# adaLN block (attention, then a gated spatial MLP): where the second half of the modulation vector is computed

## The chip, the cores and the metric

The kernel runs on one core of a Trainium2 chip. The metric is the time of one execution on the device in microseconds. All data are float32; TensorE is fed with float32 and with a rounded float32 form (F32R) of the same size.

## The reference, cut to what matters

Six modulation vectors of 448 numbers come from one vector `c` and one matrix; they scale and shift the two layer norms and gate the two branches:

```python
mod = (_silu(c) @ w_mod).reshape(c.shape[0], 6, 1, -1)        # c: 1x448, w_mod: 448x2688
sa, ca, ga, sb, cb, gb = (mod[:, i] for i in range(6))
h = _layernorm(x) * (1 + ca) + sa                             # x: 1x2048x448
x = x + ga * attention(h, A_wqkv, A_wo)                       # 16 heads of 28, 2048 keys
h = _layernorm(x) * (1 + cb) + sb
x = x + gb * gmlp(h, B_w_in, B_w_sp, B_b_sp, B_w_out)         # w_sp: 2048x2048
```

`sa` and `ca` are needed before anything else can be computed. `ga` is multiplied into the rows of `A_wo`, `gb` into those of `B_w_out`, and `sb`, `cb` are needed by the second norm, behind the attention.

## The kernel before

The order of the work is written out by hand: each engine runs its instructions in the order in which the program issues them, and semaphores join the engines. SP (SyncE) issues nearly all loads and stores, in one queue. The stages, by the time of the profile, are these.

**QKV, 0 to about 150 us.** The first norm's columns `sa`, `ca` (tiles `cols`, one column for each 128 channels, channel on the partition) are made from the first third of `w_mod` (`load_mod_chunk`, `mod_sum`, `mod_mul`, `mod_add`, `mod_prod`). Then, for four groups of 512 tokens, `ln_next` transposes the normed tokens, `v_tile` makes the values of 128 tokens, and `qk_unit` makes 128 rows of q and k for a group and sends them to memory (`qk_store` on SP). The other two thirds of `w_mod` are loaded by `load_mod` (pairs 1 and 2; four tiles of 112x896 each, SP). `mod_acc` on VectorE multiplies each of the four tiles with its column of `silu` and adds them up in `acc`, 112 channels on the partitions. What is left is a sum over 112 partitions, made on TensorE with a matrix of ones: `mod_bc` (L261) gives a gate as a row on all 128 partitions, which VectorE copies to `bcs`, and `mod_col` (L256) gives a column tile, five small matmuls, which VectorE copies to `cols`. Pair 1 (`ga`, `sb`) is finished in group 2, between two `v_tile`; pair 2 (`cb`, `gb`) behind the last `v_tile`. Each takes a bank of PSUM from the ring by `bank("pc")`: without a kind, a bank is of kind "s" (three banks) or "m" (four), by a counter `turn` that goes round seven places. The heads' tiles are three pairs, `kst` and `qst` (`stk`); `pads` clears their padding rows on VectorE and GpSimd (L545 to L547), then `load_head` reads a head back from memory. In the rest of the stage `qk_unit` runs with `m_first` in between, which begins the attention's maxima.

**Attention, about 150 to 870 us.** The loop over `u` has 16 heads of 16 slots; a slot is one block of 128 keys of a head. It is

```python
for u in range(NU + 1):
    for fn, a in events.pop(u, []):
        fn(*a)
    j = u + LEAD
    for qb in range(4 if u < NU else 0):
        s_mm(u, qb)
        if j < NU:
            m_mm(j, qb)
    if u % 2 == 0 and u > 0:
        pv_mm(u - 2)
        pv_mm(u - 1)
```

`s_mm` (L637) is one score tile of 128x512 on TensorE, in a bank of kind "s", and its Exp on ScalarE (L641), which reads the bank. `m_mm` (L607) is a product 20 slots ahead whose row maximum VectorE takes (L612), in a bank of kind "m". Since a kind's banks are used in turn, a score waits for the Exp of the score three before it. `pv_mm` (L652) multiplies the exponentials with the values, for two slots at once, behind each even slot. So one round is an odd slot, an even slot and then P times V.

What else happens in attention hangs on `events`: `at(slot, fn, ...)` issues `fn` ahead of the scores of that slot, in the order of the `at` calls. Before the change these are the loading of heads, the division by the softmax's sums (`n_copy` to `n_scatter`), the sums of blocks of `w_sp` (`ws_load` on SP, `ws_add` on GpSimd three slots later, L780, `ws_store`), the gated `A_wo` (`wo_load` from slot 120, `wo_prep` on GpSimd from slot 124 multiplies with `bcs["ga"]`), and the gated `B_w_out` (`wout_raw` from slot 196, `wout_prep` from slot 199 multiplies with `bcs["gb"]`). The tiles of `stage2` named "ql" have two buffers, used by `qk_unit`, then by `wo_load` and `wout_raw`. ScalarE has Exp alone in nearly all of attention; `qk_rest` at slot 3 puts one copy (L337) there.

**Behind it,** 870 to 1399 us: the output projection, the second norm (it reads `cols["sb"]`, `cols["cb"]`), the gated MLP with its large product with `w_sp`, and the output. The change doesn't touch these.

Of the kernel before, what the change touches and what calls it, by code (L numbers as in the profile page):

```python
# [30 lines left out]


@with_exitstack
def tile_adaln_mha_gmlp(ctx, tc, x, wqkv, wo, w_in, w_spT, b_sp, w_out, cT, w_mod, out):
# [129 lines left out]
    def bank(name, kind=None):  # L164

        if kind is None:
            kind = "smsmsmm"[turn[0] % 7]
            turn[0] += 1
        return ring.tile([128, 512], F32, name=name, tag=kind, bufs=3 if kind == "s" else 4)

    def load_mod(pair, eng):
        for k in range(4):
            wms[pair, k] = e1.tile([112, 2, D], F32, name="wm", tag=("wm", "wm", "raw")[pair], bufs=4)
            a = (pair * 4 + k) * 2 * D
            eng.dma_start(wms[pair, k], w_mod[:, a : a + 2 * D].rearrange("p (a b) -> p a b", b=D))

    def load_mod_chunk(c, eng):
        n = 128 if c < 3 else 64
        if c in (0, 2):
            ts = [e1.tile([112, 2 * D], F32, name="wm", tag="wm", bufs=4)[:, :512] for _ in range(2)]  # L180
        elif c == 1:
            ts = [stage.tile([128, 512], F32, name="wmc", tag="qh")[0:112] for _ in range(2)]
        else:
            ts = [stage2.tile([128, 512], F32, name="wmc", tag="ql")[0:112]]
        wms[0, c] = []
        a = c * 1024
        for t in ts:
            eng.dma_start(t, w_mod[:, a : a + 512])
            wms[0, c] += [t[:, j : j + 2 * n] for j in range(0, 512, 2 * n)]
            a += 512  # L190

    def load_x(g, eng):
        xg = e1.tile([128, 4, D], F32, name="xg")
        for t0, t1 in ((0, 1), (1, 2), (2, 4)) if g == 0 else ((0, 4),):
            eng.dma_start(xg[:, t0:t1, :], x[g, :, t0:t1])
        for t in range(4):
            xts[4 * g + t] = xg[:, t, :]
# [44 lines left out]
    accs = {}  # L242

    def mod_acc(pair, k):
        if k == 0:
            accs[pair] = e2.tile([112, 2, D], F32, name="acc")
        wm, acc = wms.pop((pair, k)), accs[pair]
        if k == 0:
            dve.tensor_scalar(out=acc, in0=wm, scalar1=silu[:, 0:1], scalar2=None, op0=ALU.mult)
        else:  # L250
            dve.scalar_tensor_tensor(out=acc, in0=wm, scalar=silu[:, k : k + 1], in1=acc, op0=ALU.mult, op1=ALU.add)

    def mod_col(nm, acc, plus1):
        pc = bank("pc")
        for c, r, e in ((0, 0, 128), (1, 0, 128), (2, 0, 128), (3, 0, 64), (3, 64, 128)):
            pe.matmul(pc[r:e, c : c + 1], acc[:, c * 128 : c * 128 + e - r], ones[:112, 0:1], start=True, stop=True)  # L256
        dve.tensor_scalar(out=cols[nm], in0=pc[:, 0:4], scalar1=plus1, scalar2=None, op0=ALU.add)

    def mod_bc(nm, acc):
        pc = bank("pc")  # L260
        pe.matmul(pc[:, :D], ones[:112, :], acc, start=True, stop=True)  # L261
        dve.tensor_copy(bcs[nm], pc[:, :D])

    mv1, xn1 = {}, {}

# [236 lines left out]
        qk_part("a", i, pool)  # L502
    for i in (0, 2, 1, 3):
        load_w("b", i, sp)
    load_mod(1, sp)
    for a in pvs:
        v_copy(*a)
    ln_stat(1, (0, 1))
# [3 lines left out]
    ln_rs(1, 2, 4)  # L512
    ln_norm(1, (2, 3))
    load_x(3, sp)
    ln_stat(2, range(4))
    turn[0] = 5
    qk_unit((0, 3), 0)
# [13 lines left out]
    qk_unit((2,), 0)  # L531
    for i in (0, 2, 1, 3):
        qk_part("b", i, dve)
    load_mod(2, sp)
    for g in range(1, NG):
        if g == 3:
            early.close()
            stk = att.enter_context(tc.tile_pool(name="stk", bufs=1))
            kq = [[stk.tile([128, S], F32R, name=f"{n}st{i}") for n in "kq"] for i in range(3)]
            kst, qst = [a[0] for a in kq], [a[1] for a in kq]  # L540
            npool = att.enter_context(tc.tile_pool(name="npool", bufs=2))

            def pads(i, eng):

                dve.memset(kst[i][64:128, :].bitcast(F32), 0.0)  # L545
                eng.memset(qst[i][64:128, :].bitcast(F32), 0.0)
                pool.memset(kst[i][64:86, :].bitcast(F32), 1.0)  # L547

            pads(0, dve)

            def load_head(h, c0=0, c1=S):
                k, q = kst[h % 3], qst[h % 3]
                if h > 2:
                    sp.dma_start(q[84:86, :].bitcast(F32), q[86:88, :].bitcast(F32))
                for r0, i in ((0, 0), (56, 1), (28, 0)):
                    sp.dma_start(k[r0 : r0 + 28, c0:c1].bitcast(F32), qk_scr[i][D + h * DH : D + (h + 1) * DH, c0:c1])
                for r0, i in ((0, 0), (28, 1), (56, 0)):
                    sp.dma_start(q[r0 : r0 + 28, c0:c1].bitcast(F32), qk_scr[i][h * DH : (h + 1) * DH, c0:c1])

            load_head(0, 0, 1536)  # L560
            for m in (0, 3):
                qk_unit((m,), g)
            load_head(0, 1536, S)
        v_tile(4 * g)
        v_tile(4 * g + 1)
        if g == 3:
            pads(1, pool)
            pads(2, pool)
        if g + 1 < NG:
            ln_next(g + 1)  # L570
        for k in range(2):
            v_tile(4 * g + 2 + k)
            if g == 2 and k == 0:
                mod_bc("ga", accs[1][:, 0, :])
                mod_col("sb", accs[1][:, 1, :], 0.0)
            if g < 3:
                mod_acc(g, k)
        if g < 3:
            for k, m in enumerate((0, 3)):
                qk_unit((m,), g)  # L580
                mod_acc(g, 2 + k)
    mod_col("cb", accs[2][:, 0, :], 1.0)
    mod_bc("gb", accs[2][:, 1, :])
    late_e.close()


# [202 lines left out]
    def at(slot, fn, *a, when=events):  # L789
        when.setdefault(slot, []).append((fn, a))  # L790
# [639 lines left out]
```

## Time and profile before

| what | us |
|---|---|
| median of 3 runs | 1400.98 (1400.81 to 1401.15) |
| the profiled execution, its own time | 1400.88 |
| span in it, first to last instruction | 1399.0 |
| TensorE busy | 1392.6 |
| VectorE busy | 1019.4 |
| ScalarE busy | 774.9 |
| GpSimd busy | 289.1 |

The profile's times are those of one execution. PE is TensorE's matmuls, PEld its weight loads, DVE VectorE, ACT ScalarE, POOL GpSimd, SPq the queue of SP. A row of a timeline is start, duration, engine, line, operation, output <- inputs, shape, count, and in brackets the idle time ahead of it with what ended it. A row of the chain is start, duration, engine, what was written, line, count.

### The profile page before, as it was taken

To read this page: it belongs to the slowest core of one execution; us is meant where nothing else is said; L and a number is where in the kernel's file an instruction comes from. 1 tells how busy PE (TensorE), PEld (TensorE's weight loads), DVE (VectorE), ACT (ScalarE), POOL (GpSimd) and SP (SyncE) were. 2 spreads that over 40 slices of the span, in tenths; PEclk is the share of its full clock that TensorE was granted. 3 is DMA by queue.
4 is the path that set the end of the run, shared out by engine and by line. 5 is a ranking of instruction groups with operands and counts; after the bars stand their busy time and mean duration, and the time that the engine had idled before them with its cause. 6 is when DMAs were issued, how large, how long until landed. Compare 5 with 4: busy or idle time off the path is not lost.

```text
span 1399.0 us, 20203 instructions
## 1 busy us (share of the span) xinstructions
PE 1392.6 (100%) x7208; PEld 992.1 (71%) x7208; DVE 1019.4 (73%) x1747; ACT 774.9 (55%) x1491; POOL 289.1 (21%) x275
## 2 busy tenths in 40 slices
PE   9999999999999999999999999999999999999998
PEld 8888655555555555555555555988998888888888
DVE  7788888888888888888888860751356655767473
ACT  5623666677777777666677779363234544434211
POOL 3043212211224143313211231000142430000000
PEclk9999999999999999999999999999999999999999
DMA  9563645555456546654434211534103333446453
GB/s 262 153 194 148 184 116 166 168 162 161 151 168 176 150 164 182 177 161 147 120 94 113 63 50 54 179 115 140 53 0 114 106 112 113 144 136 215 136 177 107
DMA packets 102669, 193.43 MB, mean 138 GB/s; under 512 B 17110, under 2 KB 32086, under 8 KB 100022
## 3 DMA queue, kind: packets, MB, share of 16 engines
q1 hardware_dynamic: 100138, 188.30, 44.4%
q10 hardware_dynamic: 2430, 3.84, 0.7%
q8 instruction: 57, 0.93, 0.3%
q14 instruction: 44, 0.36, 0.1%
HBM read 133.63 MB, written 53.67 MB: 134 GB/s over the span
## 4 chain that ended last, share of the span: by engine, by line
PE 99%; DVE 1%; ACT 0%; issue 0%; POOL 0%; POOLq 0%
PE st_ps L637 18%; PE o_ps L652 17%; PE mt L607 17%; PE acc L1204 6%; PE acc L1206 6%; PE acc L1205 6%; PE z_ps L1130 5%; PE z_ps L1016 5%; PE pq L313 5%; PE wo_ps L886 3%; PE pv L298 2%; PE y_ps L1306 2%; PE y_ps L1305 2%; PE y_ps L1307 2%; PE tp L118 1%; PE wu L240 1%
## 5 line engine op out<-in xcount | busy, mean ns | idle before, releaser
L612 DVE TENSOR_REDUCE pm<-mt 128x1 f32<-128x512 f32 x1024 | 631.0, 680 | 84.4 <-PE mt L607 83.9
L641 ACT ACTIVATE P<-st_ps 128x512 f32<-128x512 f32 x1024 | 514.4, 633 | 205.0 <-PE st_ps L637 205.0
L637 PE MATMUL st_ps<-qst,kst 128*128 128x512 f32 x1024 | 404.2, 406 | 0.2 <-DVE qf L319 0.2
L607 PE MATMUL mt<-kst,qst 128*128 128x512 f32 x1024 | 402.8, 393 | 0.1
L637 PEld LDWEIGHTS st_ps<-qst,kst 128*128 128x128 f32 x1024 | 191.3, 188 | 137.9 <-issue 93.9
L652 PE MATMUL o_ps<-P,V 128*32 128x512 f32 x2048 | 247.1, 598 | 0.0
L607 PEld LDWEIGHTS mt<-kst,qst 128*128 128x128 f32 x1024 | 192.4, 188 | 36.1 <-DVE pm L612 3.1
L780 POOL TENSOR_TENSOR ws_raw<-ws_raw 128x512 f32<-128x512 f32 x80 | 103.0, 1288 | 356.8 <-DMA ws_raw<-in_w_spT_dram 355.0
L1092 ACT ACTIVATE wsp_h<-raw_sp 128x512 fp32r<-128x512 f32 x112 | 70.2, 632 | 162.8 <-PE acc L1206 118.8
L85 DVE TENSOR_TENSOR wsp_l<-raw_sp,wsp_h 128x512 fp32r<-128x512 f32 x112 | 80.5, 729 | 90.6 <-ACT wsp_h L1092 87.8
L652 PEld LDWEIGHTS o_ps<-P,V 128*32 128x32 f32 x2048 | 54.7, 109 | 122.9 <-issue 114.6
L1204 PE MATMUL acc<-wsp_h,heapA 128*128 128x512 f32 x224 | 87.3, 390 | 0.0
L1205 PE MATMUL acc<-wsp_l,heapA 128*128 128x512 f32 x224 | 87.2, 389 | 0.0
L1206 PE MATMUL acc<-wsp_h,heapA 128*128 128x512 f32 x224 | 87.2, 389 | 0.0
L1205 PE MATMUL acc<-wsp_l,heapB 128*128 128x512 f32 x174 | 67.7, 389 | 0.0
L1206 PE MATMUL acc<-wsp_h,heapB 128*128 128x512 f32 x174 | 67.7, 389 | 0.0
L1204 PE MATMUL acc<-wsp_h,heapB 128*128 128x512 f32 x174 | 67.7, 389 | 0.0
L313 PE MATMUL pq<-heapD,heapD 128*128 128x512 f32 x196 | 62.4, 392 | 0.0
L1134 DVE BATCH_NORM_STATS2 stz<-z 128x6 f32<-128x448 f32 x32 | 19.9, 625 | 50.4 <-ACT z L1133 30.0
L1204 PEld LDWEIGHTS acc<-wsp_h,heapA 128*128 128x128 f32 x224 | 42.0, 188 | 8.9 <-DVE cD L1210 0.3
L1206 PEld LDWEIGHTS acc<-wsp_h,heapA 128*128 128x128 f32 x224 | 42.0, 188 | 8.8
L1205 PEld LDWEIGHTS acc<-wsp_l,heapA 128*128 128x128 f32 x224 | 42.0, 188 | 8.6
(219 smaller groups left out, 1595.4 us busy)
## 6 DMA issues: line engine op xcount, KB each, us to landing
ws_raw<-in_w_spT_dram SPq DMA_DIRECT2D x160, 256.0 KB
ws_scr<-ws_raw SPq DMA_DIRECT2D x80, 256.0 KB
raw_sp<-ws_scr SPq DMA_DIRECT2D x80, 256.0 KB
kst<-qk_scr SPq DMA_DIRECT2D x45, 224.0 KB
qst<-qk_scr SPq DMA_DIRECT2D x45, 224.0 KB
raw_sp<-in_w_spT_dram SPq DMA_DIRECT2D x32, 256.0 KB
qk_scr<-qh SPq DMA_DIRECT2D x28, 256.0 KB
qk_scr<-ql SPq DMA_DIRECT2D x28, 256.0 KB
```

The source lines that it names most:

```text
L85: eng.tensor_tensor(out=dst, in0=a, in1=hi.bitcast(F32), op=ALU.subtract)
L313: pe.matmul(pq, wqk[:, b, m * 128 : (m + 1) * 128], hT[g][:, a, :], start=j == 0, stop=j == NST - 1)
L607: pe.matmul(mt, qst[h % 3][:, t * 128 : (t + 1) * 128], kst[h % 3][:, kb * 512 : (kb + 1) * 512], start=True, stop=True)
L612: dve.tensor_reduce(out=pms[h][:, t, kb : kb + 1], in_=mt, axis=AX.X, op=ALU.max)
L637: pe.matmul(st, kst[h % 3][:, kt * 128 : (kt + 1) * 128], qst[h % 3][:, qb * 512 : (qb + 1) * 512], start=True, stop=True)
L641: act.activation(p, st, AF.Exp, scale=SCALE)
L652: pe.matmul(otile[h][32 * qb : 32 * qb + 32, :], V[:, kt, h, :], ptiles.pop((u, qb)), start=kt == 0, stop=kt == NT - 1)
L780: pool.tensor_tensor(out=a, in0=a, in1=b, op=SUMS[i // 16][2])
L1092: act.activation(hi, raw, AF.Copy)
L1204: pe.matmul(acc[i], zh, hi, start=st == 0, stop=False)
L1205: pe.matmul(acc[i], zh, lo, start=False, stop=False)
L1206: pe.matmul(acc[i], zl, hi, start=False, stop=st == 7)
```

## The change

`load_mod`, `mod_acc`, `mod_col` and `mod_bc` go, with all their calls; at the two places where `mod_bc` and `mod_col` took banks the counter goes on by 2. The four late vectors are made in attention instead. The host lays out their part of `w_mod` with channels on the rows: for each of `gb`, `sb`, `cb`, `ga` four tiles of 128 channels by 448 inputs (the last has its 64 channels twice). Early in QKV, SP writes `silu` to memory and reads it back as a row on all 128 partitions, into the tile of `bcs["ga"]`. In attention, for tile `i` of 16: at slot 8 + 6i SP loads it into a "ql" buffer, at slot 12 + 6i GpSimd multiplies it with the row, and at slot 16 + 6i ScalarE copies it in place and gives the sum along each row, which is one column of the vector. `sb` goes straight to `cols["sb"]`; GpSimd adds 1 to `cb`; the two gates are written to memory and read back as rows (SP; `gb` at slot 36 and `ga` at slot 108). Their column tiles are those of `sa` and `ca`.

```diff
-    def load_mod(pair, eng):
-        for k in range(4):
-            wms[pair, k] = e1.tile([112, 2, D], F32, name="wm", tag=("wm", "wm", "raw")[pair], bufs=4)
-            a = (pair * 4 + k) * 2 * D
-            eng.dma_start(wms[pair, k], w_mod[:, a : a + 2 * D].rearrange("p (a b) -> p a b", b=D))
...
+    def row(i):
+        return m_scr[0, i, 0:D].rearrange("(o n) -> o n", o=1).broadcast_to([128, D])
...
-    def mod_acc(pair, k):
...
-    def mod_col(nm, acc, plus1):
...
-    def mod_bc(nm, acc):
...
-    load_mod(1, sp)
...
     load_x(3, sp)
+    sp.dma_start(m_scr[0, 0, 0:D].rearrange("(k p) -> p k", p=112), silu)
+    sp.dma_start(bcs["ga"], row(0))
...
-    load_mod(2, sp)
...
         for k in range(2):
             v_tile(4 * g + 2 + k)
             if g == 2 and k == 0:
-                mod_bc("ga", accs[1][:, 0, :])
-                mod_col("sb", accs[1][:, 1, :], 0.0)
-            if g < 3:
-                mod_acc(g, k)
+                turn[0] += 2
         if g < 3:
-            for k, m in enumerate((0, 3)):
+            for m in (0, 3):
                 qk_unit((m,), g)
-                mod_acc(g, 2 + k)
-    mod_col("cb", accs[2][:, 0, :], 1.0)
-    mod_bc("gb", accs[2][:, 1, :])
+    turn[0] += 2
...
+    LATE = ("gb", "sb", "cb", "ga")
+    gcols = {"sb": cols["sb"], "cb": cols["cb"], "gb": cols["sa"], "ga": cols["ca"]}
+    mods = {}
+
+    def mod_load(i):
+        mods[i] = stage2.tile([128, D], F32, name="w_late", tag="ql")
+        sp.dma_start(mods[i], w_late[i])
+
+    def mod_mult(i):
+        pool.tensor_tensor(out=mods[i], in0=mods[i], in1=bcs["ga"], op=ALU.mult)
+
+    def mod_sum_row(i):
+        nm, c = LATE[i // 4], i % 4
+        m = mods.pop(i)
+        act.activation(m, m, AF.Copy, accum_out=gcols[nm][:, c : c + 1])
+
+    def mod_end(nm):
+        if nm == "cb":
+            pool.tensor_scalar(out=cols[nm], in0=cols[nm], scalar1=1.0, scalar2=None, op0=ALU.add)
+        elif nm != "sb":
+            g, r = gcols[nm], m_scr[0, 1, 0:D]
+            sp.dma_start(r[0:384].rearrange("(c p) -> p c", p=128), g[:, 0:3])
+            sp.dma_start(r[384:D].rearrange("(c p) -> p c", p=64), g[0:64, 3:4])
+            sp.dma_start(bcs[nm], row(1))
...
+    for i in range(16):
+        at(8 + 6 * i, mod_load, i)
+        at(12 + 6 * i, mod_mult, i)
+        at(16 + 6 * i, mod_sum_row, i)
+    for i, nm in enumerate(LATE):
+        at(36 + 24 * i, mod_end, nm)
```

The number of output elements, of heads and of slots stays as it was; so does every line of the stages behind attention.

More of the change, by code (lines that the diff above doesn't have):

```diff
@@ L33, in tile_adaln_mha_gmlp @@
 @with_exitstack
-def tile_adaln_mha_gmlp(ctx, tc, x, wqkv, wo, w_in, w_spT, b_sp, w_out, cT, w_mod, out):
+def tile_adaln_mha_gmlp(ctx, tc, x, wqkv, wo, w_in, w_spT, b_sp, w_out, cT, w_mod, w_late, out):
     nc = tc.nc
@@ L240, in pe_fill @@
             pe.matmul(wu[:, 0:128], with_[:, 0:128], ones, start=True, stop=True)
-    accs = {}
-    def mod_acc(pair, k):
[L245 to L251, printed above, removed]
-    def mod_col(nm, acc, plus1):
[L254 to L257, printed above, removed]
-    def mod_bc(nm, acc):
-        pc = bank("pc")
-        pe.matmul(pc[:, :D], ones[:112, :], acc, start=True, stop=True)
-        dve.tensor_copy(bcs[nm], pc[:, :D])
     mv1, xn1 = {}, {}
@@ L1401 @@
     from concourse.bass_utils import run_bass_kernel_spmd as _run
-    wm = _np.asarray(inputs["w_mod"]).reshape(4, 112, 3, 2, 448).transpose(1, 2, 0, 3, 4)
-    w_mod = _np.concatenate(
-        [wm[:, 0, :, :, c : c + 128].reshape(112, -1) for c in (0, 128, 256, 384)] + [wm[:, 1:].reshape(112, -1)], axis=1
-    )
+    wm = _np.asarray(inputs["w_mod"]).reshape(448, 6, 448)
+    first = wm[:, 0:2].reshape(4, 112, 2, 448).transpose(1, 0, 2, 3)
+    w_mod = _np.concatenate([first[..., c : c + 128].reshape(112, -1) for c in (0, 128, 256, 384)], axis=1)
+    rows = _np.concatenate([_np.arange(448), _np.arange(384, 448)])
+    w_late = wm[:, [5, 3, 4, 2]].transpose(1, 2, 0)[:, rows].reshape(16, 128, 448)
     lay = {
@@ L1416 @@
         "w_mod": w_mod,
+        "w_late": w_late,
     }
```

## The prediction

> **What bounds the kernel now.** I read the page's head and its chain of work that ended last first.
>
> ```profile
> span 1399.0 us, 20203 instructions
> PE 1392.6 (100%) x7208; PEld 992.1 (71%) x7208; DVE 1019.4 (73%) x1747; ACT 774.9 (55%) x1491; POOL 289.1 (21%) x275
> PE 99%; DVE 1%; ACT 0%; issue 0%; POOL 0%; POOLq 0%
> ```
>
> TensorE carries 99% of the chain, so the span changes by what TensorE gains or loses. The reader should distrust two things here: a TensorE busy all the time may still be waiting for very short times, because ends of matmuls are modelled, and ScalarE's 55% is a mean over stages. So the next views are the chain and the timeline at the two places that the change touches: 55 to 92 us, where the products leave TensorE, and a piece of attention, where the row sums go in. The chain, window 55 to 92 us (start, us, what):
>
> ```profile
> 59.58 2.24 PE pv L298 x11
> 61.81 0.76 PE pc L261 x2
> 62.57 0.77 PE pc L256 x10
> 63.34 2.44 PE pv L298 x11
> 65.78 10.02 PE pq L313 x44
> 75.81 8.96 PE pv L298 x44
> 84.77 0.78 PE pc L256 x10
> 85.55 0.95 PE pc L261 x2
> 86.49 0.23 PE pq L313
> ```
>
> There is no other engine in it: the products (L261, L256) stand as pieces of TensorE's own time. In attention, the chain (first two rows of its kind) and the timelines of ScalarE and VectorE show a fixed rhythm:
>
> ```profile
> 403.80 1.85 PE o_ps L652 x16
> 409.55 1.85 PE o_ps L652 x16
> ```
> ```profile
> 400.37 4.03 ACT L641 ACTIVATE P<-st_ps 128x512 f32<-128x512 f32 x8 [1.72 <-PE st_ps L637]
> 406.12 4.03 ACT L641 ACTIVATE P<-st_ps 128x512 f32<-128x512 f32 x8 [1.72 <-PE st_ps L637]
> ```
> ```profile
> 400.60 4.87 DVE L612 TENSOR_REDUCE pm<-mt 128x1 f32<-128x512 f32 x8 [0.87 <-PE mt L607]
> ```
>
> Every two slots take 409.55 - 403.80 = 5.75 us: a burst of eight scores (L637), eight products for the row maxima (L607), then P times V (L652). ScalarE makes its eight Exp in 4.03 us and rests 1.72. (Which slots these are will matter below: the burst at 158.87, quoted there, is that of slots 3 and 4, and 42 bursts of 5.75 later is 400.37, so this is the burst of slots 87 and 88.) It looks as if ScalarE had room. Whether it has room inside the burst is decided by the scores' banks: three of kind "s", so the eighth score can only be loaded when the fifth Exp has ended, the seventh after the fourth. Four close looks at one burst: weight loads on TensorE, then the fourth Exp, then the fifth.
>
> ```profile
> 402.26 0.19 PEld L607 LDWEIGHTS mt<-kst,qst 128*128 128x128 f32 x1
> 402.49 0.19 PEld L637 LDWEIGHTS st_ps<-qst,kst 128*128 128x128 f32 x1
> 402.71 0.19 PEld L607 LDWEIGHTS mt<-kst,qst 128*128 128x128 f32 x1
> 402.98 0.19 PEld L637 LDWEIGHTS st_ps<-qst,kst 128*128 128x128 f32 x1
> ```
> ```profile
> 401.82 0.62 ACT L641 ACTIVATE P<-st_ps 128x512 f32<-128x512 f32 x1
> ```
> ```profile
> 402.30 0.63 ACT L641 ACTIVATE P<-st_ps 128x512 f32<-128x512 f32 x1
> ```
>
> The fourth Exp ends at 401.82 + 0.62 = 402.44 and the seventh score's load begins 0.05 later; the fifth ends at 402.93 and the eighth load begins at 402.98, again 0.05 later. That last load comes 0.08 after the load before it ended (402.71 + 0.19), the seventh 0.04 after its own. So TensorE already waits some 0.04 us for ScalarE at the end of the burst. **ScalarE's slack in the middle of a burst is nothing**, though it is idle 30% of the time. This is the fact on which the forecast rests.
>
> **The change part by part.**
>
> *Removed from TensorE.* Without the products the two value tiles that take 2.24 us each (59.58, and 63.34 less its start-up) would follow directly: 65.78 - 59.58 - 2 x 2.24 = 1.72 us. At the second place 86.49 - 84.77 = 1.72 us. Together **-3.44 us**. Is the second 1.72 collected? The first product for the maxima (L607, 86.6 us) needs head 0 back from memory, and that load waits for pads made by VectorE:
>
> ```profile
> 72.10 1.14 DVE L251 SCALAR_TENSOR_TENSOR acc<-wm,silu,acc 112x896 f32<-112x896 f32 x1
> 73.72 1.76 DVE L545 MEMSET kst<- 64x2048 f32 x1 [0.49 <-DVE acc L251]
> ```
>
> The pad at 73.72 waited for the accumulation before it, which goes too, so it comes at least as much earlier as TensorE does. I count the full 3.44 and keep 1.72 as the other end.
>
> *Removed elsewhere.* Eight accumulations, two row copies and two column copies on VectorE, and eight loads from SP, in a stage where TensorE never waits for them: 0. Bank turns are kept by the two steps of the counter.
>
> *Added early.* SP writes silu out and reads it back as rows while the first q and k tiles are made. SP has a wait of one write in it, and behind it stand the q and k stores, which nobody needs before head 0 is loaded at 74 us: 0. If that cover were gone, one landing, about the 2.9 us that I take below for such a wait.
>
> *Added in attention, off the bound.* Per sixth slot one load on SP and one product on GpSimd. GpSimd's time by size from the row below is 1.30 x 448/512 = 1.14 us, 16 of them 18 us in 276 us where its page share is 21%. The product doesn't slow VectorE's maxima: their 4.87 us above stands beside the sum at 400.31. The question is only whether each product is ready for its sum.
>
> ```profile
> 396.05 0.81 SPq L776 DMA_DIRECT2D ws_raw<-in_w_spT_dram  x2
> ```
> ```profile
> 400.31 1.30 POOL L780 TENSOR_TENSOR ws_raw<-ws_raw 128x512 f32<-128x512 f32 x1 [3.52 <-DMA ws_raw<-in_w_spT_dram]
> ```
>
> From issue to the operation that uses a load of twice the bytes: 4.26 us. A slot is 5.75/2 = 2.87 us; SP runs up to about two slots late: this pair belongs to slot 84, two bursts before slot 88, whose first Exp begins at 402.30, so near 390.8, and it was issued 5.3 us behind that. Load to product has four slots (11.5 us) and product to sum another four: 5.7 + 4.3 + 1.1 = 11.1 of 23 us. SP's write-and-read of a finished gate, at slots 36 and 108, holds SP for a landing; its nearest row, in the view of SP's waits (in total, times, longest), is
>
> ```profile
> SPq L678 <- DMA r_scr<-rt: 7.3, 4, 2.9
> ```
>
> 2.9 us at most, behind which stand weight-sum loads, head loads (ten slots ahead of use) and the next load: still inside 23 us. GpSimd's addition of 1 to a column tile has four elements a partition. Together 0.
>
> *Added in attention, on ScalarE.* Each of the 16 sums is queued at slot 16 + 6i, always even, ahead of that slot's Exp. A burst is an odd slot and then an even one, P times V behind it, so the sum stands **between the fourth and fifth Exp**, the place without slack. Behind it queue the fifth to eighth Exp, and the eighth score waits for the fifth. Each sum therefore delays TensorE by its whole length X, and the rest of ScalarE after the burst doesn't give it back, because the next burst starts from TensorE's end. What is X? Rows of ScalarE early in the span:
>
> ```profile
> 12.23 0.56 ACT L342 ACTIVATE wv<-raw 128x448 fp32r<-128x448 f32 x1
> 12.70 0.25 ACT L413 ACTIVATE col_ca<-pc,ones 128x1 f32<-128x1 f32 x1
> 12.84 0.16 ACT L414 ACTIVATE col_sa<-pc 128x1 f32<-128x1 f32 x1
> ...
> 17.27 0.56 ACT L342 ACTIVATE wv<-raw 128x448 fp32r<-128x448 f32 x1
> 17.74 0.39 ACT L384 ACTIVATE acc<-wmc,silu 112x128 f32<-112x128 f32 x1
> ```
>
> A 128x448 copy from SBUF to SBUF lets the next instruction start 0.47 us later. The row sum has no row here: the trace holds no activation with a sum. It can't be nothing or below, since the sum has to pass 448 elements through the engine, and the fastest pace here is the Exp's own, by size 0.49 x 448/512 = 0.43 us (0.49 is (4.03 - 0.63)/7, an Exp lasting 0.63), so X is at least 0.43. Its upper end is a copy that overlaps nothing and a read-out that costs the longer 128x1 row: 0.56 + 0.25 = 0.81. I take 0.47 plus a read-out between the two 128x1 rows (0.16, 0.25), 0.21, because a sum can be written only after its last element: X = 0.68. 16 x 0.68 = **+10.9 us**.
>
> Copy between Exps: the trace has one, at slot 3, in the rest after a burst, and the page of groups has two table loads in all, neither in attention.
>
> ```profile
> 156.71 0.62 ACT L337 ACTIVATE qh<-qf 128x512 fp32r<-128x512 f32 x1
> 158.87 4.03 ACT L641 ACTIVATE P<-st_ps 128x512 f32<-128x512 f32 x8 [1.53 <-PE st_ps L637]
> ```
> ```profile
> L230 ACT ACT_TABLE_LOAD x1 | 1.3, 1283 | 0.7 <-PEq L1418 0.7
> L1020 ACT ACT_TABLE_LOAD x1 | 1.3, 1283 | 0.0
> ```
>
> That copy cost nothing (the next burst again takes 4.03), as it stood where ScalarE rests. The Trainium skill, "Perfetto Trace Analysis", section "Matmuls", says that matmul groups should go round different PSUM banks so that emptying one overlaps the next group's matmuls. By that rule the sums would be hidden under the 1.72 us of rest; the trace agrees only in so far as the banks suffice, and three do not in the burst (0.05 us behind the Exp).
>
> *Sum:* 1400.9 (the profiled execution's own time, 1399.0 of span and 1.9 around it) - 3.4 + 10.9 = 1408.4 us. The runs' median, 1400.98, is 0.1 from that execution, so the forecast stands for both.
>
> **The rivals.**
>
> *The banks leave room* (the other side). The mechanism is the ring of score banks: if the eighth score could start before the fifth Exp ends, the sum would go into ScalarE's rest and only -3.4 stays: 1397.5. It decides at a slack of X; half a slack gives a time within 0.2%. For it: 1.72 us of rest per burst, and the harmless copy at slot 3. Against it: the two distances of 0.05 us. 8% in full, 4% in part (X under 0.39, where 16 X - 3.4 is under 2.8).
>
> *The gain is not collected.* The chunk before 86 us ends on head 0's load instead: half of the gain goes, 1400.9 - 1.7 + 10.9 = 1410.1. Against it: the pad row above. 6%.
>
> *Late products.* SP's order, with its new waits on ScalarE and on a written gate, brings loads later than 23 us, and ScalarE waits inside a burst. With one slot each for the five sums nearest to SP's late slots: 5 x 2.9 = 14.5 more, 1422.9. For it: SP is two slots late already at places. Against: 12 us in hand. 5%.
>
> *Table loads.* Were Copy and Exp in two sets, each sum would cost two loads: 32 x 1.28 = 41 us, 1449. Against it: slot 3 has none. 1%.
>
> **How the numbers follow.** The forecast has 76%. Its ends: 16 x 0.43 - 3.4 = +3.5, 1404.4; and 16 x 0.81 - 1.7 = +11.3, 1412.2, which takes in the uncollected gain. That range holds 82%. A measurement of this kernel tells about 0.2%, 2.8 us, from no change. Faster 8%, within 4%, slower 88% (76 + 6 + 5 + 1).
>
> **What would show it.** Right: rows of the sum on ScalarE at even slots with nothing of L251, L256, L261 before 90 us; P times V beginning 0.7 us later in 16 bursts, the eighth score's load right behind the fifth Exp in each, and the other bursts at 5.75. The chain would name ScalarE for pieces in these bursts. The first score, whose row is here, should start 3.4 us earlier; 1.7 would mean the uncollected gain.
>
> ```profile
> L637 PE MATMUL st_ps<-qst,kst x1024: 387/393/504, 149.9 to 866.0; 128*128 128x512 f32 x171
> ```
>
> Late products would show as ScalarE idle before the sum with GpSimd as the releaser. Wrong: the 16 bursts as long as the others, or a sum shorter than 0.43 us.

## The result, and the profile after

| kernel | median us | runs |
|---|---|---|
| before | 1400.89 | 4, 1400.66 to 1401.15 |
| changed | 1423.03 | 4, 1420.17 to 1427.25 |

The changed kernel takes 1.016 times the time of before (95% interval 1.0128 to 1.0192). The sign was as forecast, the size was not: 22 us more, not 7.5. The profiled execution of the changed kernel took 1420.33 us, so its span stands 19.5 us above that of before. The page's head and its shares of the chain that ended last:

```profile
span 1418.5 us, 20212 instructions
PE 1398.0 (99%) x7184; PEld 989.5 (70%) x7184; DVE 1012.5 (71%) x1735; ACT 784.3 (55%) x1523; POOL 309.1 (22%) x292
PE 90%; DMA 4%; ACT 3%; DVE 1%; SPq 1%; issue 1%; POOL 1%; POOLq 0%; ACTq 0%
```

TensorE carried 99% of the chain before. Now 4% of it is DMA and 1% SP, and ScalarE has only 3%. So the transfers come first below, and then the sums. (In the changed kernel a score is L632, its Exp L636, a value tile L273, a q or k row L288.)

I put the start of each slot's first score side by side in the two traces and went through the differences:

| where | us | what |
|---|---|---|
| 42 to 57 us, first stage | +8.7 | one stop |
| 57 us to the first score | -3.4 | products gone from TensorE |
| slots 17, 23, ... 107 | +7.0 | 16 steps of 0.44, the sums |
| slots 45 to 48 | +3.4 | one stretch, beside a sum's step |
| slot 112 | +2.7 | one step |
| behind attention | +1.2 | small pieces, see below |

**The stop.** TensorE's timeline from 42 us, first of the kernel before, then of the changed one:

```profile
41.93 1.91 PE L118 MATMUL tp<-ident,xn 128*128 128x128 f32 x16
43.60 4.74 PE L298 MATMUL pv<-wv,heapD 128*128 128x448 f32 x22
48.17 0.86 PE L313 MATMUL pq<-heapD,heapD 128*128 128x512 f32 x3
```
```profile
42.00 1.47 PE L118 MATMUL tp<-ident,xn 128*128 128x128 f32 x12
49.14 1.11 PE L118 MATMUL tp<-ident,xn 128*128 128x128 f32 x4 [5.66 <-DVE ql L85]
50.73 6.29 PE L273 MATMUL pv<-wv,heapD 128*128 128x448 f32 x22 [0.47 <-DVE ql L85]
56.85 0.39 PE L288 MATMUL pq<-heapD,heapD 128*128 128x512 f32 x1
```

The two kernels are level at 42 us and 8.7 apart at the next q row. TensorE sits idle for 5.66 and 0.47 us, and the 22 value matmuls behind that take 6.29 us instead of 4.74. The chain of waits of the changed kernel names what stands behind VectorE's `ql`:

```profile
31.18 10.82 DMA m_scr<-silu
...
42.01 0.33 SPq L490
...
43.38 5.57 DMA qk_scr<-qh
```

Read from below: TensorE waited for VectorE's `ql`, and the chain goes from that through ScalarE's `qh` to the store of a `qh`: neither engine could go on with q and k while their buffers were still being stored. Those stores were issued late because SP stood at L490 with the read of silu; and that read waited 10.8 us for the write of silu, 1.8 KB. Not all of this is the write's own: the load of `x` (896 KB) was issued 0.4 us ahead of it in the same queue, and silu_write_16B below shows how much of the wait passes with that load.

**The removal.** The same chain of the changed kernel at the two places where the products were:

```profile
68.28 4.49 PE pv L273 x22
72.77 10.02 PE pq L288 x44
82.79 8.97 PE pv L273 x44
91.76 0.23 PE pq L288
```

The 22 value matmuls up to the 44 of q and k take 4.49 us, where from 59.58 to 65.78 us before it was 6.20: 1.71 us gone. At the end 91.76 - 82.79 = 8.97 against 86.49 - 75.81 = 10.68, again 1.71.

**A sum.** ScalarE's timeline in one burst, then the last weight loads of that burst on TensorE:

```profile
414.38 2.07 ACT L636 ACTIVATE P<-st_ps 128x512 f32<-128x512 f32 x4 [1.72 <-PE st_ps L632]
416.30 0.60 ACT L616 ACTIVATE w_late<-w_late 128x448 f32<-128x448 f32 x1
416.77 0.22 ACT L616 ACTIVATION_READ_ACCUMULATOR w_late<-w_late 128x1 f32 x1
416.86 2.08 ACT L636 ACTIVATE P<-st_ps 128x512 f32<-128x512 f32 x4
```
```profile
417.53 0.19 PEld L632 LDWEIGHTS st_ps<-qst,kst 128*128 128x128 f32 x1 [0.61 <-ACT P L636]
417.64 0.19 PEld L577 LDWEIGHTS mt<-kst,qst 128*128 128x128 f32 x1
```

The sum stands between the fourth and the fifth Exp, and the eighth score's load waits 0.61 us for the fifth Exp. The sum costs ScalarE 416.86 - 416.30 = 0.56 us: the read-out of 0.22 starts 0.47 behind it and the next Exp 0.09 behind the read-out's start, so the Exp overlaps most of the read-out. TensorE then follows with the next load 0.11 us behind instead of the usual 0.23, which gives back 0.1 of it; the step is 0.44. The view of waits over 160 to 500 us counts all of them:

```profile
PEld st_ps L632 <- ACT P L636: 9.5, 16, 0.6
```

**The gates.** SP's two longest waits on one transfer in attention (200 to 520 us; total, times, longest) and the chain behind the first of them:

```profile
SPq L625 <- DMA m_scr<-col_ca: 9.3, 1, 9.3
SPq L625 <- DMA m_scr<-col_sa: 8.3, 1, 8.3
```
```profile
265.78 8.86 DMA m_scr<-col_sa
...
275.57 8.21 DMA rb<-r_scr
...
294.89 3.05 DMA qst<-nf
...
298.08 0.47 PE st_ps L632
```

The read of the finished gate holds SP for 8.3 us, the row of softmax sums `rb` behind it lands 8.2 us after its issue, and the rest of that head's queue is late until the maxima `nf` of the next head reach their tile `qst`: TensorE waits for them at slot 48. One of the added products (1.15 us on GpSimd, L611) stands in this chain too, behind the product with `rb`.

### The profile page after: what moved, and what is told of

Read it like the earlier page. It is cut to its first block, busy times and chain, and to the rows that moved or that the text cites. A ratio compares the mean times of both kernels' runs of the same rounds, so it can differ in the third digit from the quotient of the medians.

```text
span 1418.5 us, 20212 instructions
## 1 busy us (share of the span) xinstructions
PE 1398.0 (99%) x7184; PEld 989.5 (70%) x7184; DVE 1012.5 (71%) x1735; ACT 784.3 (55%) x1523; POOL 309.1 (22%) x292
## 4 chain that ended last, share of the span: by engine, by line
PE 90%; DMA 4%; ACT 3%; DVE 1%; SPq 1%; issue 1%; POOL 1%; POOLq 0%; ACTq 0%
PE st_ps L632 16%; PE o_ps L647 16%; PE mt L577 14%; PE acc L1205 6%; PE acc L1207 6%; PE acc L1206 6%; PE z_ps L1131 5%; PE z_ps L1017 5%; PE pq L288 4%; ACT P L636 3%; PE wo_ps L887 3%; PE pv L273 2%; PE y_ps L1307 2%; PE y_ps L1308 2%; PE y_ps L1306 2%; DMA m_scr<-silu 1%
## 5 line engine op out<-in xcount | busy, mean ns | idle before, releaser
L636 ACT ACTIVATE P<-st_ps 128x512 f32<-128x512 f32 x1024 | 516.8, 629 | 208.8 <-PE st_ps L632 208.8
L632 PE MATMUL st_ps<-qst,kst 128*128 128x512 f32 x1024 | 406.1, 408 | 7.7 <-DMA qst<-nf 4.6
L632 PEld LDWEIGHTS st_ps<-qst,kst 128*128 128x128 f32 x1024 | 191.3, 188 | 150.6 <-issue 99.3
L288 PE MATMUL pq<-heapD,heapD 128*128 128x512 f32 x196 | 62.1, 390 | 0.0
```

Source lines behind the costliest of these rows:

```text
L288: pe.matmul(pq, wqk[:, b, m * 128 : (m + 1) * 128], hT[g][:, a, :], start=j == 0, stop=j == NST - 1)
L632: pe.matmul(st, kst[h % 3][:, kt * 128 : (kt + 1) * 128], qst[h % 3][:, qb * 512 : (qb + 1) * 512], start=True, stop=True)
L636: act.activation(p, st, AF.Exp, scale=SCALE)
```

## The experiments

Theory A: the detours through memory cost so much because small writes hold SP and the transfers behind them; the sums cost 0.44 us each because of their place. Each edit is against the changed kernel where nothing else is said. Where no number of runs is given there was one; the four runs of the changed kernel lie 7 us apart, so the steps in the profile say more than such a single time. The runs of before beside them had medians of 1400.7 (the first four), 1401.46 (the next four), 1401.42 (small_pieces_moved, silu_write_16B) and 1400.44 (the last two).

### silu_read_late: SP no longer waits for silu

```diff
     sp.dma_start(m_scr[0, 0, 0:D].rearrange("(k p) -> p k", p=112), silu)
-    sp.dma_start(bcs["ga"], row(0))
...
     load_head(1)
+    sp.dma_start(bcs["ga"], row(0))
```

> One move: SP reads silu's row back behind head 1's load (near 90 us) and not right behind its write at 31 us; the write stays. Theory A (SP, waiting in its queue for the landing of the small write, holds back the q and k stores, their two buffers stay full, and TensorE stops): the stop of 5.9 us ahead of the transposes near 49 us goes, the first score starts at 146.5 to 147.5 us and not at 155.2, and the whole is 8 to 9 us shorter than the changed kernel, 1411 to 1414. Rival B (the loss of that stage is the added traffic itself, or work that VectorE and GpSimd do in another order): write and read are still there, so the first score stays within 1.5 us of 155.2.

1418.46 us in one run; the first score came at 152.43, between the two theories. SP's wait is gone, but TensorE still sits idle for 3.6 us there, against 6.1. The chain:

```profile
31.38 13.96 DMA qk_scr<-qh
```

The q store issued right behind the small write, without any wait in SP, lands 14 us later (here too the load of `x` stands ahead of both). So the write delays what stands behind it in two ways: through SP when SP waits for it, and in the transfers themselves when it does not.

### sums_odd_slots: the sums moved by one slot

```diff
-        at(16 + 6 * i, mod_sum_row, i)
+        at(17 + 6 * i, mod_sum_row, i)
```

> One move: the 16 row sums on ScalarE are issued one slot later, at odd slots, so ahead of the first Exp of a burst and not between the fourth and the fifth. Theory A (a sum costs TensorE time only in the middle of a burst, where the banks of the scores leave no slack; after P times V ScalarE rests 1.72 us): the 16 steps of 0.44 us go, about 7 us, no burst of slots 17 to 107 waits for an Exp longer than before the change. Rival B (each sum's 0.56 us of ScalarE is paid wherever it stands, or the product on GpSimd is what the burst waits for): the steps stay at 0.3 to 0.6 us each, in another place of the burst.

1417.03 us. All 16 steps are gone. ScalarE around one sum:

```profile
411.60 4.03 ACT L636 ACTIVATE P<-st_ps 128x512 f32<-128x512 f32 x8 [1.72 <-PE st_ps L632]
415.43 0.65 ACT L616 ACTIVATE w_late<-w_late 128x448 f32<-128x448 f32 x1
415.90 0.27 ACT L616 ACTIVATION_READ_ACCUMULATOR w_late<-w_late 128x1 f32 x1
417.35 1.09 ACT L636 ACTIVATE P<-st_ps 128x512 f32<-128x512 f32 x2 [1.19 <-PE st_ps L632]
```

Ahead of an odd slot the sum stands where ScalarE rests: eight Exp run through in 4.03 us, and 1.19 us of idle time is left behind the read-out. In this execution the gates' stretches were dearer (5.7 us at slots 48 and 49 and 5.0 at 112 and 113, against 3.4 and 2.7), each with a stretch of half clock behind its stop: the granted clock was 0.50 from 297.5 to 300.9 us and 0.51 from 485.2 to 488.6 us, where the changed kernel had 1.00. So the span fell by 3.3 and not by 7.0.

### gate_read_late: the gates read nine slots after they are written

```diff
-            sp.dma_start(bcs[nm], row(1))
+    def mod_read(nm):
+        sp.dma_start(bcs[nm], row(1))
...
+        if nm in ("gb", "ga"):
+            at(45 + 24 * i, mod_read, nm)
```

> One move: the two finished gates are read back as rows nine slots behind their writes (slots 45 and 117) and not right behind them (36 and 108); the writes stay. Theory A (SP waits 8 to 9 us for the small writes and then reaches the store of the negated maxima late, for which the next head's scores wait): the extra steps at slots 45 to 48 (3.4 us) and 112 (2.7 us) go, about 6 us in all. Rival B (the writes' 448 elements of 4 bytes hold up the loads of heads and blocks by themselves): the steps stay.

1415.03 us. The stretch at slots 45 to 48 is gone, and the step at slot 112 is down from 2.7 to 0.6. No sum stands there (the last is at slot 106); TensorE waits 0.5 us for `nf`. So most of what the gates' detour cost here came from SP waiting in it, and a rest at slot 112 stays without that wait.

### three_moves: the three edits above together

> All three moves at once. Theory A (three separate losses, each undone by its own move, and a gain of 3.4 us from the products that left TensorE): 1397 to 1399 us, faster than the kernel before by 2 to 4 us. Rival B (a loss moves on to the next wait when one is undone, or the added loads and products cost something themselves): 1400 or more.

Four runs had a median of 1406.39 us (1405.43 to 1406.93), 1.0043 times before (1.0026 to 1.006). Attention is flat but for 0.6 us at slots 126 and 127, and the first score is still 4.0 us later than before. The view of TensorE's waits from 30 to 60 us, and behind it a stretch of the engines' busy times (PE, PEld, DVE, ACT, POOL, each with its instructions; then granted clock, DMA share, GB/s):

```profile
PE tp L118 <- DVE ql L85: 3.5, 1, 3.5
```
```profile
49.00:52.00 3.00, 3.00 (x10) 2.65 (x9) 2.93 (x8) 2.97 (x6) 0.00 (x0) 0.50 0.49 185
```

The full recovery that theory A promised failed: the small write alone, with nobody waiting for it, still stops TensorE. The next four runs ask why.

### four_moves: silu also written later

Against three_moves:

```diff
-    sp.dma_start(m_scr[0, 0, 0:D].rearrange("(k p) -> p k", p=112), silu)
...
+        if g == 1:
+            sp.dma_start(m_scr[0, 0, 0:D].rearrange("(k p) -> p k", p=112), silu)
```

> The three moves, and silu's small write itself moved from 31 us to behind the q and k stores of the second group (near 58 us), where SP has some 11 us without a store. What the earlier runs left: with only the read moved, the q store issued right behind the small write still landed 14 us later. Theory A (the small write holds up whatever lies behind it among the DMAs for about 10 us, whether or not SP waits; TensorE stops when that is a q or k store): no stop near 45 us, first score at 146.5, 1397 to 1398 us in all, faster than before by 3 to 4. Rival B (the stop near 45 us comes from the stores of the first group being late for another reason, such as the load of x ahead of them): the stop of about 4 us stays, 1403 to 1406.

1399.91 us in 11 runs (1398.79 to 1401.68), 0.9986 times before (0.9977 to 0.9995), above the range of theory A. Written behind the stores of group 1, the same pieces make no stop in the first stage, and the first score comes 2.2 us earlier than before. Of the 1.2 us that are missing from 3.4, the start-up of this execution has 0.6; the other 0.6 are lost near 115 us, as in every profile here in which silu is read back behind head 1's load. What remains are 1.3 us at slots 47 and 48, where the write of `gb` makes the next head's `nf` late, and 0.3 at slot 112.

### three_moves_16B: silu written at its old place in fewer pieces

Against three_moves:

```diff
-    sp.dma_start(m_scr[0, 0, 0:D].rearrange("(k p) -> p k", p=112), silu)
+    sp.dma_start(m_scr[0, 0, 0:D].rearrange("(p k) -> p k", k=4), silu)
```

The host puts the inputs in each row of `w_late` into the same order.

> The three moves, with silu's write at 31 us in another layout: four numbers of a partition side by side, so 112 pieces of 16 bytes in place of 448 of 4; the matrix is laid out on the host to fit. Theory A (each piece costs the same, so the holding goes with their number): the q store behind it lands after some 4 us and not 14, TensorE stops less than 1 us near 45 us, 1398 to 1400. Rival B (any small write to memory costs about 10 us): like the three moves alone, the stop of about 4 us stays, 1403 to 1406.

1399.44 us, first score 3.2 us earlier than before. TensorE in the same window:

```profile
42.00:49.00 7.00, 7.00 (x42) 6.44 (x41) 6.46 (x16) 5.84 (x12) 1.41 (x2) 1.00 0.40 150
```

It is busy in all of it. The same bytes, from the same place, in 112 pieces of 16 bytes instead of 448 of 4, leave no stop there. The gates, still in pieces of 4 bytes, cost 1.0 us at slot 48.

### three_moves_act_queue: silu written from ScalarE's queue

Against three_moves, `sp.dma_start` becomes `act.dma_start` in that line.

> The three moves, with silu's write at 31 us issued from ScalarE's queue and not from SP's; 448 pieces of 4 bytes as before. Theory A (the holding is an order within one queue): the q store behind it lands in 3 to 5 us, no stop near 45 us, 1397 to 1399. Rival B (the pieces occupy the engines that all queues share): the stop stays, 1403 to 1406.

1402.56 us. TensorE's wait for `ql` is 1.7 us instead of 3.5, and from 36 to 42 us the DMA engines are seen fully busy (1.00) at 60 GB/s. So in this one run neither pure reading holds: part of the harm goes with SP's queue, part reaches transfers of another queue.

### products_left_out: nothing in place of what was removed

```diff
+    for late_tile in (cols["sb"], cols["cb"], bcs["gb"], bcs["ga"]):
+        pool.memset(late_tile, 1.0)
...
-    sp.dma_start(m_scr[0, 0, 0:D].rearrange("(k p) -> p k", p=112), silu)
-    sp.dma_start(bcs["ga"], row(0))
...
-    for i in range(16):
-        at(8 + 6 * i, mod_load, i)
-        at(12 + 6 * i, mod_mult, i)
-        at(16 + 6 * i, mod_sum_row, i)
-    for i, nm in enumerate(LATE):
-        at(36 + 24 * i, mod_end, nm)
```

> The removal alone: the late vectors are not computed at all (gates and the second norm's columns are set to 1), so there is no write or read of silu, no load, product, sum or gate in attention. It measures the step of -3.4 us of the forecast by itself. Theory A: first score at 146.5, 1397.5 us. Rival B (part of it is not collected, because head 0 is not loaded in time): first score at 147.5 to 149, 1398.5 to 1400.

1399.43 us, in the range of rival B. But the first score came 3.0 us earlier than before; the start-up ran 0.5 us late in this execution, and from the first q row of group 1 on the gain is 3.5. The last stage took 0.9 us more than in the profile of before. The changed kernel's does too, so that piece does not come from the late vectors.

### small_pieces_moved: silu in 16-byte pieces behind group 1, the gates written behind the maxima

Against four_moves: silu as in three_moves_16B with its read right behind the write, and

```diff
-    for i, nm in enumerate(LATE):
-        at(36 + 24 * i, mod_end, nm)
+    for nm, slot in (("gb", 45), ("sb", 60), ("cb", 84), ("ga", 109)):
+        at(slot, mod_end, nm)
         if nm in ("gb", "ga"):
-            at(45 + 24 * i, mod_read, nm)
+            at(slot + 9, mod_read, nm)
```

> silu is written in 112 pieces of 16 bytes and read back at the end of group 1, the sums stand at odd slots, the gates are written at slots 45 and 109 and read nine slots later. Theory A (every loss of the change was a DMA that held SP or the queues, or a sum in mid-burst): no stop near 45 us, first score near 146.5 us (3.4 earlier than before), no step over 0.3 us at slots 45 to 48 and 112; 1396.5 to 1398.5 us, 2 to 4 us faster than before. Rival (the gates' writes in 4-byte pieces hold up whatever stands behind them, wherever they stand): steps of about 1 us come back near slots 57 and 121, or the reads near 60 us delay the q and k stores; 1399 to 1402 us.

1401.13 us in 12 runs (1399.15 to 1405.87), 1.0002 times before (0.9993 to 1.001). The first stage is as theory A has it (first score 146.79), but the rival is right about the gates: in the profiled execution (1404.09 us, above the median) 4.0 us are lost at slots 64 and 65 and 1.7 at slots 125 to 127. The loads of `w_sp` that GpSimd waits for (last number in brackets) stand right behind the gate's write. Nine of the twelve runs lie at 1402.2 us or below, so most executions can't have lost all of this. GpSimd of this kernel:

```profile
292.11 1.28 POOL L778 TENSOR_TENSOR ws_raw<-ws_raw 128x512 f32<-128x512 f32 x1 [13.63 <-DMA ws_raw<-in_w_spT_dram]
```

And the same sum in the kernel before:

```profile
286.62 1.30 POOL L780 TENSOR_TENSOR ws_raw<-ws_raw 128x512 f32<-128x512 f32 x1 [6.66 <-DMA ws_raw<-in_w_spT_dram]
```

SP does not wait for the gate there; the large load behind its 448 pieces is 7 us late by itself, and SP's queue stays late for one head.

### silu_write_16B: the landing by itself

The changed kernel with the one edit of three_moves_16B; the read stays right behind the write, so that SP shows the landing.

> The changed kernel with one edit: silu is written as 112 pieces of 16 bytes in place of 448 of 4, and read back right behind it as in the changed kernel, so that SP's wait shows the landing. Theory A (the landing goes with the number of pieces): the read is issued 3 to 5 us behind the write in place of 10.8, TensorE's stop in the first stage is under 1 us, the first score comes 6 to 8 us earlier than in the changed kernel (147 to 149 us), and the time is 1411 to 1414 us. Rival (a small write to memory costs 8 to 10 us whatever its pieces): read and first score as in the changed kernel, about 155 us, and 1418 to 1422 us.

1409.49 us, 1.5 below the foot of theory A's range. SP's timeline:

```profile
31.13 0.42 SPq L489 DMA_DIRECT2D m_scr<-silu  x1
35.48 0.33 SPq L490 DMA_DIRECT2D bc_ga<-m_scr  x1
```

The read follows 4.35 us behind the write, against 10.83 in the changed kernel, and the first score comes at 147.30 against 155.23. In both kernels the load of `x` stands ahead of the write. The stretches of the changed kernel, and then the first one of this run (the last number is GB/s):

```profile
31.00:35.20 4.20, 4.20 (x28) 3.76 (x27) 4.03 (x11) 3.63 (x7) 1.28 (x2) 1.00 0.70 219
35.20:42.00 6.80, 6.80 (x33) 5.93 (x33) 4.19 (x8) 3.74 (x8) 0.00 (x0) 1.00 0.02 2
```
```profile
31.00:35.20 4.20, 4.20 (x28) 3.73 (x26) 4.03 (x11) 3.59 (x7) 1.28 (x2) 1.00 0.65 219
```

By 35.2 us 219 GB/s x 4.2 us, or 0.92 MB, have moved in either, which is the load. From there SP gets on after 0.3 us with the 16-byte pieces and after 6.8 with the 4-byte ones, while next to nothing is seen moving. So about 4 us of both waits pass while the load still moves, and the two layouts differ by more than 4.35 and 10.83 say. One line of layout is worth about 8 us there. The gates, still in 4-byte pieces, keep 4.0 us of steps (6.1 in the changed kernel, with the same code there, so these steps are not equal in every execution).

### gates_16B_moved: the gates in 16-byte pieces too

Against small_pieces_moved. The host gives each gate's four tiles every fourth channel, so that a partition holds four neighbouring channels and one transfer does for two:

```diff
-            sp.dma_start(r[0:384].rearrange("(c p) -> p c", p=128), g[:, 0:3])
-            sp.dma_start(r[384:D].rearrange("(c p) -> p c", p=64), g[0:64, 3:4])
+            sp.dma_start(r.rearrange("(p k) -> p k", k=4), g[0:112, :])
```

> As small_pieces_moved, but each gate too is written in one transfer of 112 pieces of 16 bytes instead of 448 of 4 (its tiles hold every fourth channel). Theory A (the loads behind a gate's write were held by its many small pieces): the load of w_sp behind the write lands within 6 us instead of 15, no idle time of TensorE ahead of slot 64, no step over 0.3 us between slots 45 and 66 and between 109 and 128; 1396.5 to 1398.5 us, faster than before by 0.2 to 0.35%. Rival (SP's queue is late there for the late vectors' own loads and the two more transfers, whatever the pieces): the step of about 4 us at slots 64 and 65 stays at 2 us or more; 1400 to 1402 us.

1398.15 us in 11 runs (1396.84 to 1399.07), 0.9982 times before (0.9973 to 0.9991). GpSimd's wait at the place shown above:

```profile
284.45 1.29 POOL L777 TENSOR_TENSOR ws_raw<-ws_raw 128x512 f32<-128x512 f32 x1 [6.47 <-DMA ws_raw<-in_w_spT_dram]
```

It is as short as in the kernel before, and slot 64 no longer waits. This version is the fastest of those that compute everything, 0.18% under before (the interval of four_moves, 0.14% under, overlaps with this one's). A step of 1.0 us is left at slots 61 to 63, which theory A had excluded; TensorE waits there for VectorE's maxima, and I didn't follow it.

### pieces_alone: every place kept, only the pieces changed

Both layout edits on the changed kernel: silu as in silu_write_16B, the gates as in gates_16B_moved, all at their old slots with the reads right behind the writes.

> The changed kernel with every place and order kept, but silu and the two gates written in 112 pieces of 16 bytes each. Theory A (the pieces, not the places, made the detours dear): first score near 147.3 us as in silu_write_16B, SP's wait for a written gate under 5 us instead of 8.3 and 9.3, steps at slots 45 to 48 and at 112 together under 1.5 us beyond the sums (4.0 in silu_write_16B), the 16 sums at 0.44 us each; 1405.5 to 1407.5 us. Rival (SP's wait in the heads' loads costs the same at any length over 4 us): steps as in silu_write_16B, 1409 to 1410 us.

1405.45 us. SP's waits, in the first stage and then in attention:

```profile
SPq L490 <- DMA m_scr<-silu: 3.8, 1, 3.8
```
```profile
SPq L624 <- DMA m_scr<-col_ca: 3.8, 1, 3.8
SPq L624 <- DMA m_scr<-col_sa: 2.4, 1, 2.4
```

The first score comes 2.5 us earlier than before, the 16 sums cost 0.44 each, slots 45 to 48 and 112 show no step of their own, and the span ends 4.7 us above before: -2.5 + 16 x 0.44 = +4.5. With the pieces enlarged, SP's waits at the same places do no harm that the slots show; in the first stage a wait of 0.4 us for `ql` is left, and 0.7 us are lost by the first q row of group 1. For silu only the layout differs. For a gate the edit also makes one transfer out of two, and no run separates that from the size of the pieces.

## Why the prediction failed where it did

**Removed from TensorE, -3.44: right.** 1.71 us at each of the two places, and 3.4 at both together in products_left_out. The gain was collected in full; the rival of a gain not collected falls.

**Added early, "0", and without the cover one landing of 2.9: wrong, by 8.7 us.** This is the step that failed most. I saw SP's wait and asked only who needs the q and k stores' data at the other end (head 0, at 74 us). Their sources need them too: `qh` and `ql` are buffers that ScalarE and VectorE refill, and these were the ones that ran out. And the landing was not 2.9 us but 10.8, of which about 4 passed while the load of `x` ahead of it in the queue still moved. The row that I took, `r_scr<-rt`, was the landing of a different transfer; silu's layout in memory, one element of 4 bytes at a time, was in the diff, and I didn't look at it. silu_write_16B and three_moves_16B show that this layout is the cause.

**SP's write-and-read of a gate, 2.9 us at most, "together 0": wrong, by 6.1 us.** The same mistake: 8.3 and 9.3 us, for pieces of 4 bytes as well. The loads of the late vectors did have their 23 us; I tested the wait against these alone and waved the rest through. What came late were the sums' rows `rb` and, behind them, the next head's `nf`. With waits of 2.4 and 3.8 us (pieces_alone) the slots show no loss: near the 2.9 us that I took the step comes out right, but a wait of 2.9 didn't apply to this write.

**Added in attention on ScalarE: right in mechanism and place, X too large.** The sums cost TensorE at even slots, by the eighth score's wait for the fifth Exp, and nothing at odd ones. X was 0.68 and came out at 0.44, so the term is 7.0 and not 10.9. I added the read-out (0.21) in full behind the copy (0.47); the next Exp overlaps it, so ScalarE loses 0.56, and TensorE makes up 0.1 behind the late load. The foot of my bound, 0.43, was the nearer end.

**Products, the addition of 1, tables: right, 0.** Nothing was late:

```profile
L616 ACT ACTIVATE w_late<-w_late 128x448 f32<-128x448 f32 x16 | 9.6, 597 | 0.0
```

The idle time ahead of the 16 sums is 0.0 us. So the rival of late products fell, although its time, 1422.9, lies next to the measured one: it named SP's waits on a written gate rightly, but its price came from ScalarE waiting for GpSimd, which does not happen in this execution. A matching number was no support for its mechanism. The rival in which the banks leave room falls with the 16 waits.

**The sum.** By the steps of the profile it is -3.4 + 8.7 + 7.0 + 6.1 + 1.2 = 19.6 us, against 19.5 measured in that execution. With X at 0.44 and everything else as I had it: 1400.9 - 3.4 + 7.0 = 1404.5. pieces_alone, which is the change without its 4-byte pieces, took 1405.45; of the 1.0 us between them 0.7 are lost in the first stage, as said there, and 0.3 are a later start-up of that execution. The profiled execution of the changed kernel took 15 us more than pieces_alone: 8 up to the first score, 6 at slots 45 to 48 and 112, and 1 behind attention. The first two are the 4-byte pieces and what they hold up, with the reserve on the gates made above. The last is a slower last stage that some executions show and others don't, without the late vectors too; its cause stays open.

Open stays in part why four runs of the changed kernel lie up to 7 us apart, where the four of before are within half a microsecond (in the later sets of 7 to 16 runs, within 2.1). The runs of 1420.17 and 1420.33 us had mean granted clocks of 0.997 and 0.998, those of 1425.73 and 1427.25 us 0.994 and 0.991. So the longer ones ran for longer at a lowered clock, as sums_odd_slots did behind the gates' stops; where they did, no profile of them shows.

## What to carry to other kernels

A small transfer is not priced by its bytes: here the same 1.8 KB kept SP waiting 6.8 us behind the load of `x` in pieces of 4 bytes, and 0.3 us in pieces of 16. Look up the layout on both sides of every small DMA that a change adds, and give each partition its neighbours so that a piece is longer than one element. When a DMA queue gets a new wait, list not only the readers of what is queued behind it but also the buffers that those stores free. A long instruction that shares an engine with a tight ring belongs in the rest of the ring's cycle; one slot's difference was worth 7 us here, twice what taking the products from TensorE had brought.

## What I had not expected of the hardware

**A write of 448 pieces of 4 bytes holds up its surroundings.** It landed 10.8 us after its issue (8.3 to 9.3 us of waiting for the gates), and without a wait a store behind it landed after 14 us; 112 pieces of 16 bytes took 4.35 from write to read. Counted from 35.2 us, when the load of `x` was through, it was 6.8 against 0.3 us. The number of pieces alone doesn't explain it. In silu_write_16B, from 39 to 40 us,

```profile
DMA packets 225, 0.41 MB, mean 407 GB/s; under 512 B 26, under 2 KB 27, under 8 KB 225
```

225 packets went through in one microsecond, 198 of them of 2 to 8 KB; at that pace 448 would take 2 us, an estimate. So it matters that the pieces are short; how the price falls between 4 and 16 bytes, no run shows. In the changed kernel the 16 DMA engines were hardly seen busy while SP waited:

```profile
36.00:42.00 6.00, 6.00 (x30) 5.29 (x29) 3.39 (x7) 3.40 (x8) 0.00 (x0) 1.00 0.02 3
```

In silu_read_late, where the stores were let loose behind the write, they were nearly full (0.87) and moved 32 GB/s, where a row of the next paragraph has 325 GB/s at 0.89:

```profile
36.00:42.00 6.00, 6.00 (x32) 5.37 (x31) 3.16 (x6) 3.09 (x8) 0.00 (x0) 1.00 0.87 32
```

What the engines do with the pieces, no view shows. The Trainium skill, "DMA: Bandwidth & Descriptors", section "Latency and other measured facts", says that a tiny transfer to and from memory can't go below about 800 ns whatever its size; no run here shows that floor. The write of 4-byte pieces lay far above it, and at equal size it fell with the layout alone.

**After a stop TensorE runs at half clock for a while.** In the changed kernel, with the granted clock third from the end:

```profile
42.00:49.00 7.00, 1.48 (x13) 1.23 (x11) 0.61 (x1) 0.60 (x1) 0.00 (x0) 0.88 0.81 179
49.00:52.00 3.00, 2.39 (x7) 1.87 (x8) 2.10 (x6) 2.65 (x7) 0.00 (x0) 0.50 0.89 325
52.00:60.00 8.00, 8.00 (x34) 7.00 (x33) 6.28 (x15) 5.78 (x10) 1.89 (x2) 0.87 0.03 13
```

The time missing from full clock, (0.12 x 7 + 0.50 x 3 + 0.13 x 8) / 0.50, is 6.8 us at half clock. The 1.7 us before 49 us fall into the stop itself; the other 5.1 us cost TensorE 2.5 us of work. So 6.1 us of idle time cost 8.7. A wait of 1.7 us (three_moves_act_queue) left the clock at 1.00. The Trainium skill, "TensorE: Matmul & The Clock Gate", Part 1, has a clock that falls to half after an idle window of some 3.4 us and comes back after one of work; the trace agrees, with 6.8 us at half where the stop was 5.7 (the half clock begins near 47.3 us, 3.8 behind the start of the stop), and the row of three_moves above, behind a stop of 3.5 us, shows 0.50 too.
